# Turning more probability tiles by DVE and DRAM instead of TensorE, in a top-k attention and GELU kernel

## The chip, the cores and the metric

The kernel runs on 1 core of one Trainium2 chip. A core has five engines with a queue of instructions each, worked in order: TensorE (PE in the profile, its weight loads PEld), VectorE (DVE), ScalarE (ACT), GpSimd (POOL) and SyncE (SP, which here only issues DMAs). [...] The metric is device microseconds of one execution: the kernel before takes 1480.06 us (median of 3 runs, 1479.93 to 1480.07).

## The reference

Attention over 8 batches of 8 heads, 576 rows of 64 columns each, in which each row keeps its 32 largest scores; the heads of a batch are laid side by side and go through two products with an exact GELU between them. All is float32.

```python
scores = scale * np.matmul(q, k.transpose(0, 1, 3, 2))     # (8, 8, 576, 576)
kth = np.partition(scores, -32, axis=-1)[..., -32:-31]
scores = np.where(scores >= kth, scores, -1000000000.0)
scores = scores - np.max(scores, axis=-1, keepdims=True)
attn = np.exp(scores)
attn = attn / (np.sum(attn, axis=-1, keepdims=True) + 1e-09)
out = np.matmul(attn, v)
x = out.transpose(0, 2, 1, 3).reshape(4608, 512)
h = x @ w_in                                                # 512 x 2048
g = 0.5 * h * (1.0 + erf(h * inv_sqrt2))
return g @ w_out                                            # 2048 x 512
```

## The kernel before, in words

**Items.** The work of attention is cut into 144 items, 18 for each batch. An item is a tile `s` of 128 rows by 2 x 576 scores. 16 items of a batch are main items: 128 query rows of a pair of heads (a pair has 4 such blocks of rows, 512 in all; two neighbouring items, an even and an odd one, share a pair). The last 64 rows of the heads are left over, and two items of last rows hold them, each for two pairs (four heads). In even batches the items of last rows stand at the end, in odd batches at the start, so they come in groups of four.

**One step.** The order of instructions is written out by hand in one loop over n, and each engine takes its share in that order. In step n the loop makes the scores of item n + 2 (in even steps of n + 2 and n + 3, lines 386 and 394), the top-k of item n, the softmax of item n - 1, the transposes of item n - 2 and the product with v (`attend`) of item n - 3. Between them stand pieces of the two big products (`mlp`), lines 773 and 929 above all; `room_in` says how many pieces a step gets. Pieces are taken in a fixed order, and only when the rows of x that they need are there.

**Top-k.** DVE finds the 32 largest of a row in four rounds of 8 (line 483), and between rounds replaces those found by a very low number (line 486). For most items the first two rounds run over 288 larger halves (line 422), the last two over 576 numbers. In step n the last thing of the top-k is `last()`, the reciprocal of the sum of the exponentials of item n - 1 (line 504); DVE waits there for ACT's exponentials (line 529) by way of a small addition on POOL (line 510). After it POOL makes the threshold of item n (lines 497 and 498), which ACT needs for its selection (line 517), and multiplies item n - 1 by the reciprocal (line 552).

**Turning P.** The product with v needs the probabilities with the keys on the partitions, so each item is turned over. An ordinary item is turned by PE: one transpose for the 2 x 64 last keys (line 619) and eight for the rest (line 649), which ACT copies from PSUM to the tile `pt` (lines 629 and 664). An item of last rows needs two end transposes (line 622) and has a small tile `pt_end` of its own. Of the even main items 48 go another way (`squared`): DVE transposes all 32 x 32 squares of the tile in place (`square_p`, line 569, in the middle of the top-k two steps later), SP writes the tile to DRAM by four DMAs (`write_p`, line 579) and reads it back by four others in the order in which whole blocks are turned (`read_p`, line 586, at the head of the next step). The reads wait until the writes have landed. There is one tile `pt` (bufs=1); the even item fills its left half, the odd one its right half, and one product (line 715) takes both, in the step after the odd item's transposes.

**Loads.** From the fifth pair of heads on q and k are loaded in squares too, by eight DMAs for each of q and k of a pair (line 124), and DVE turns them (lines 284 to 288). All DMAs of the steady part are issued by SP, in program order; `issue` holds some back behind the write of a turned tile.

**Tiles.** Six tiles of scores `s` go round, so the scores of item n + 2 need the tile of item n - 4, in even steps those of n + 3 that of n - 3.

## Time and profile before

| what | value |
|---|---|
| median of 3 runs | 1480.06 us |
| profiled execution | 1479.73 us, span 1478.0 us |
| PE busy | 1461.6 us (99%) |
| DVE busy | 1294.3 us (88%) |
| POOL busy | 1140.1 us (77%) |
| ACT busy | 1099.9 us (74%) |
| DMA packets | 477645, 112.94 MB |
| DMA, queue of SP | 35.3% of 16 engines' span |
| granted PE clock | 1.00 |

Busy time of an engine is the time in which at least one of its instructions ran; a busy PE is not PE at its peak, since the ends of matmuls are modelled and overlap the next. A matmul of the program stands as two instructions in the trace, a transpose by PE as one. A row of a group gives the line, the engine, the operation, the tile written and those read, the shape and the count, then busy time in us and the mean length of one in ns, then the time for which the engine idled before it and what ended that. A row in order of time gives start and length in us. Rows of waits say who waited for whom, how long in total, how often, and the longest.

### The profile page before, as it was taken

Reading aid. Unit: us, or ns where it says so; the run is one execution under the profiler, and the core shown is the slowest. Engines: PE = TensorE matmul, PEld = TensorE weight load, DVE = VectorE, ACT = ScalarE, POOL = GpSimd, SP = SyncE. Lnnn points to the kernel's source line nnn. Section 1 sums busy time; section 2 is a strip of 40 time slices with the busy share of each in tenths; the row PEclk is TensorE's granted clock in tenths of the full one; section 3 lists DMA queues with packets and bytes.
Section 4 is the critical chain, followed back from the end, with each engine's and each line's share of the span. In section 5 each row is a group of like instructions: output and inputs, shape, how many; then the busy total and the mean of one; then the engine's idle time right before and its main releaser. Section 6 shows DMA issues by size and latency. Waiting matters only on the chain. (4 is left out here: it accounts for less than half of the span.)

```text
span 1478.0 us, 27006 instructions
## 1 busy us (share of the span) xinstructions
PE 1461.6 (99%) x8817; PEld 1147.9 (78%) x8817; DVE 1294.3 (88%) x3318; ACT 1099.9 (74%) x1942; POOL 1140.1 (77%) x1291
## 2 busy tenths in 40 slices
PE   8999999999999999999999999999999999999999
PEld 6876677877777777887777778787777777787787
DVE  8999899999999988999999987999999997998701
ACT  7999977877777687777777778777777777776620
POOL 6877567877898879877898978886788887987732
PEclk9999999999999999999999999999999999999999
DMA  7424310045435322345534331345453421233300
GB/s 198 143 86 124 84 48 1 24 88 101 95 73 93 66 58 52 65 95 108 105 83 81 69 61 47 66 93 99 97 103 73 89 55 41 61 61 72 70 15 15
DMA packets 477645, 112.94 MB, mean 76 GB/s; under 512 B 413216, under 2 KB 469056, under 8 KB 477504
## 3 DMA queue, kind: packets, MB, share of 16 engines
q1 hardware_dynamic: 476240, 110.78, 35.3%
q8 instruction: 70, 1.15, 0.3%
q14 instruction: 71, 0.58, 0.1%
q10 hardware_dynamic: 1200, 0.39, 0.1%
q0 software_dynamic: 64, 0.03, 0.0%
HBM read 73.39 MB, written 37.75 MB: 75 GB/s over the span
## 5 line engine op out<-in xcount | busy, mean ns | idle before, releaser
L773 PE MATMUL h_ps<-xT,w_in_sb 128*128 128x256 f32 (+1 forms) x2560 | 536.2, 361 | 0.1
L773 PEld LDWEIGHTS h_ps<-xT,w_in_sb 128*128 128x128 f32 x2560 | 436.5, 190 | 73.4 <-issue 25.2
L483 DVE MAX8 top<-lists 128x8 f32<-128x576 f32 (+1 forms) x792 | 476.4, 641 | 0.0
L486 DVE MATCH_REPLACE8 lists<-top,lists 128x288 f32<-128x288 f32 (+1 forms) x528 | 307.9, 589 | 0.0
L552 POOL TENSOR_TENSOR s<-s,rden 128x1152 f32<-128x1152 f32 x135 | 285.8, 2117 | 0.3 <-DVE rden L504 0.3
L529 ACT ACTIVATE s<-s,bias 128x576 f32<-128x576 f32 x288 | 225.4, 787 | 11.0 <-issue 0.4
L517 ACT ACTIVATE s<-s,neg 128x576 f32<-128x576 f32 x288 | 225.5, 793 | 1.7 <-POOL neg L497 1.6
L510 POOL TENSOR_SCALAR den<-den 128x2 f32<-128x2 f32 x144 | 31.4, 218 | 215.9 <-ACT s L529 210.2
L455 POOL TENSOR_TENSOR lists<-lists 128x576 int32<-128x576 int32 x132 | 186.2, 1410 | 4.0
L447 POOL TENSOR_TENSOR lists<-s 128x576 int32<-128x576 int32 x133 | 187.2, 1407 | 0.0
L715 PE MATMUL o<-pt,raw_v 128*64 128x256 f32 x1280 | 153.0, 384 | 1.8 <-ACT s L529 1.1
L715 PEld LDWEIGHTS o<-pt,raw_v 128*64 128x64 f32 x1280 | 87.8, 136 | 85.8 <-issue 37.2
L789 ACT ACTIVATE g<-h_ps 128x512 f32<-128x512 f32 x144 | 78.2, 594 | 100.6 <-PE h_ps L773 100.4
L929 PE MATMUL y_ps<-w_out_sb,sum 128*128 128x256 f32 x472 | 140.4, 379 | 0.0
L394 ACT ACTIVATE s<-s_ps 128x1024 f32<-128x1024 f32 x127 | 125.5, 1035 | 10.5 <-PE s_ps L386 10.3
L664 ACT COPY pt<-tp 128x1024 f32<-128x1024 f32 x85 | 86.6, 1019 | 62.2 <-PE tp L649 62.1
L386 PE MATMUL s_ps<-kt,qm 64*128 64x512 f32 x512 | 129.4, 618 | 0.8 <-ACT s L392 0.8
L504 DVE RECIPROCAL rden<-den 128x2 f32<-128x2 f32 x144 | 23.2, 161 | 108.6 <-POOL den L510 107.4
L486 DVE MATCH_REPLACE8 lists<-first,lists 128x288 f32<-128x288 f32 x264 | 114.3, 439 | 0.0
L929 PE MATMUL y_ps<-w_out_sb,g 128*128 128x256 f32 x480 | 113.4, 379 | 0.0
L483 DVE MAX8 first<-lists 128x8 f32<-128x288 f32 x268 | 106.6, 436 | 0.0
L929 PEld LDWEIGHTS y_ps<-w_out_sb,g 128*128 128x128 f32 x480 | 91.2, 190 | 12.4
(167 smaller groups left out, 2533.1 us busy)
## 6 DMA issues: line engine op xcount, KB each, us to landing
turned<-s SPq DMA_DIRECT2D x192, 144.0 KB, 3.5
pt<-turned SPq DMA_DIRECT2D x192, 144.0 KB, 3.2
raw_v<-in_v_dram SPq DMA_DIRECT2D x64, 128.0 KB, 2.4
out_dram<-y SPq DMA_DIRECT2D x30, 256.0 KB, 2.1
raw_q<-in_q_dram SPq DMA_DIRECT2D x112, 64.0 KB, 2.0
raw_k<-in_k_dram SPq DMA_DIRECT2D x112, 64.0 KB, 2.0
w_out_sb<-in_moe_w_in_dram SPq DMA_DIRECT2D x14, 511.8 KB, 4.8
w_out_sb<-in_moe_w_out_dram SPq DMA_DIRECT2D x10, 511.8 KB, 4.1
```

Source lines behind the costliest of these rows:

```text
L386: nc.tensor.matmul(s_ps[:, e], lhsT=q_t[rows, :], rhs=kt[rows, 0:SM], start=True, stop=True)
L394: nc.scalar.activation(spread(s, S + TL, SM), s_ps, func=AF.Copy, scale=scale)
L447: nc.gpsimd.tensor_tensor(t[:, :, 1].bitcast(i32), a.bitcast(i32), b.bitcast(i32), op=ALU.add)
L455: nc.gpsimd.tensor_tensor(into_of(i)[:, :, 1].bitcast(i32), both, top, op=ALU.subtract)
L483: nc.vector.max(x[:, e], src[:, e])
L486: nc.vector.match_replace(dst[:, e], x[:, e], src[:, e], LOWEST)
L517: nc.scalar.activation(s, s, func=AF.Prelu, bias=st["neg"][:, e : e + 1], scale=1.0, alpha=STEEP)
L529: nc.scalar.activation(s, s, func=AF.Exp, bias=st["bias"][:, e : e + 1], scale=1.0, accum_out=st["den"][:, e : e + 1],)
L552: nc.gpsimd.tensor_tensor(s, s, wide, op=ALU.mult)
L715: nc.tensor.matmul(o[e * D : (e + 1) * D, 0:n], lhsT=vt[:, j, e, :], rhs=pt[:, e * NJ + j if j < NM else NM, :], start=(j == 0), stop=(j = ...
L773: nc.tensor.matmul(h_tile(u)[:, i, :], lhsT=w_in_sb[:, ko, f * P : (f + 1) * P], rhs=xT[:, ko, c0 : c0 + n], start=(ko == 0), stop=(ko == ...
L929: nc.tensor.matmul(acc[names][:, k], lhsT=lhsT, rhs=rhs, start=(j == 0 and k == 0), stop=(j == FT // 2 - 1 and k == 1),)
```

## The change

- **More items turned by DVE and DRAM.** Beside the even main items from the 27th item on, `squared` now takes all 12 later items of last rows (`delayed`) and 16 odd main items (`later`: those whose place in a period of 36 items is 3, 13, 21, 25 or 29). PE's transposes and ACT's copies of these go; DVE gets a transpose of squares, SP four writes and four reads for each.
- **A layout for that.** For pairs loaded in squares the first head's left-over keys are its first 64 and not its last 64, so that an item of last rows has the same column layout as a main item, with the left-over keys of both heads side by side; `pt_end` goes. q and k take four DMAs each, not eight.
- **The later items' chain.** In the step after a later item the reciprocal is taken before the last maximum and not after it, and POOL multiplies before it makes the threshold. The square transpose stands after the first round of the top-k and not before the third. The product with v of a later item stands at the end of its step and not at the start, and two pieces of the big products are moved from the step before into that step (`bare`).
- **The delayed items.** Their products come one or two steps later, the two groups of an odd batch share a PSUM tile and one copy, and the small loads of v behind them are issued by ACT.
- **Room.** Seven tiles `s` in place of six; small tiles are put together, `part` has two buffers, `top` 16 columns.

```diff
--- before.py
+++ after.py
@@ -118,20 +118,24 @@
             for e in range(2):
+                at = e * TL if n == "k" else 0
                 for d in range(2):
                     rows, cols = slice((2 * e + d) * SQ, (2 * e + d + 1) * SQ), slice(d * SQ, (d + 1) * SQ)
-                    for at, lo, hi, by in ((0, 0, SM, queue), (SM + e * TL, SM, S, queue2)):
-                        by.dma_start(
-                            out=t[rows, at : at + hi - lo].rearrange("i (c j) -> i c j", j=SQ),
-                            in_=src[b, h0 + e, lo:hi, cols].rearrange("(c i) j -> i c j", i=SQ),
-                        )
+                    queue.dma_start(
+                        out=t[rows, at : at + S].rearrange("i (c j) -> i c j", j=SQ),
+                        in_=src[b, h0 + e, :, cols].rearrange("(c i) j -> i c j", i=SQ),
+                    )
             return
...
         for e in range(2):
+            end = TL if pair >= SQUARES and e == 0 else S
+            main = end % S
             queue.dma_start(
-                out=t[:, 0:NM, e, :], in_=src[b, h0 + e, 0:SM].rearrange("(t p) d -> p t d", p=P)
+                out=t[:, 0:NM, e, :], in_=src[b, h0 + e, main : main + SM].rearrange("(t p) d -> p t d", p=P)
             )
-            queue2.dma_start(out=t[e * TL : (e + 1) * TL, NM, e, :], in_=src[b, h0 + e, SM:S])
+            rows = slice(0, TL) if n == "q" else slice(e * TL, (e + 1) * TL)
+            queue2.dma_start(out=t[rows, NM, e, :], in_=src[b, h0 + e, end - TL : end])
...
@@ -283,7 +287,7 @@
             elif c == 1:
-                nc.vector.transpose(kt[:, q_tail:], rq[:, SM:])
+                nc.vector.transpose(kt[:, q_tail : q_tail + TL], rq[:, SM:S])
             else:
...
@@ -312,15 +316,33 @@
             if c != 0 and done >= {1, 2}:
-                load("q", pair + ahead)
+                issue(lambda: load("q", pair + ahead))
             if (c == 0 if pair >= SQUARES else c != 0 and done >= {0, 1, 2}):
-                load("k", pair + ahead)
+                issue(lambda: load("k", pair + ahead))
...
     S_of, stat_of = {}, {}
+    def main_keys(pair):
+        return slice(TL, TL + SM) if pair >= SQUARES else slice(0, SM)
+    def end_keys(pair, e):
+        at = e * (SM + TL) if pair >= SQUARES else SM + e * TL
+        return slice(at, at + TL)
+    def both_ends(pair):
+        kt = kt_of[pair]
+        return spread(kt, SM + TL, TL) if pair >= SQUARES else kt[:, SM : SM + P]
+    def end_rows(pair, e):
+        return slice(SM + P, SM + P + TL)
...
@@ -361,21 +379,19 @@
                 nc.tensor.matmul(
-                    t_ps[half(r, e), r * TL : (r + 1) * TL],
-                    lhsT=kt[:, SM + P + e * TL : SM + P + (e + 1) * TL],
-                    rhs=kt[:, SM + e * TL : SM + (e + 1) * TL],
+                    t_ps[half(r, e), e * TL : (e + 1) * TL],
+                    lhsT=kt[:, end_rows(pair + r, e)], rhs=kt[:, end_keys(pair + r, e)],
                     start=True, stop=True,
...
         return lambda: nc.scalar.activation(
-            s.rearrange("p (r n) -> p r n", r=2)[:, :, SM:S],
-            t_ps[:, 0:P].rearrange("p (r n) -> p r n", r=2), func=AF.Copy, scale=scale,
+            s[:, SM : S + TL], t_ps[:, 0:P], func=AF.Copy, scale=scale
         )
...
         pair, t = items[i]
-        S_of[i] = s = work.tile([P, 2 * S], f32, tag="s", bufs=6, name="s")
+        S_of[i] = s = work.tile([P, 2 * S], f32, tag="s", bufs=7, name="s")
         s_ps = pair_tile("s_ps", "l1" if second else "pr")
@@ -384,7 +400,7 @@
                 nc.tensor.matmul(
-                    s_ps[:, e], lhsT=q_t[rows, :], rhs=kt[rows, 0:SM], start=True, stop=True
+                    s_ps[:, e], lhsT=q_t[rows, :], rhs=kt[rows, main_keys(pair)], start=True, stop=True
                 )
...
@@ -454,18 +469,18 @@
-    def top_k(i, last, middle):
+    def top_k(i, last, middle, early, late):
...
             "first": work.tile([P, 2, 8], f32, tag="first", name="first"),
-            "neg": work.tile([P, 2], f32, tag="neg", name="neg"),
-            "bias": work.tile([P, 2], f32, tag="bias", name="bias"),
-            "den": work.tile([P, 2], f32, tag="den", name="den"),
-            "rden": work.tile([P, 2], f32, tag="rden", name="rden"),
         }
-        top = work.tile([P, 2, TOPK - 8], f32, tag="top", bufs=1, name="top")
-        into = [st["first"]] + [top[:, :, 8 * r : 8 * r + 8] for r in range(TOPK // 8 - 1)]
+        stat = work.tile([P, 4, 2], f32, tag="stat", name="stat")
+        st.update((n, stat[:, x]) for x, n in enumerate(("neg", "bias", "den", "rden")))
+        top = work.tile([P, 2, 16], f32, tag="top", bufs=1, name="top")
+        into = [st["first"]] + [
+            top[:, :, 8:16] if r == TOPK // 8 - 1 else top[:, :, 0:8] for r in range(1, TOPK // 8)
+        ]
         if paired(i):
@@ -477,17 +492,21 @@
         for r, (src, dst, x) in enumerate(rounds):
-            if 16 * r == TOPK:
+            if 16 * r == TOPK and not late:
                 middle()
...
                 nc.vector.max(x[:, e], src[:, e])
+                if early and e == 0 and r == len(rounds) - 1:
+                    last()
+            if r == 0 and late:
+                middle()
             if r < len(rounds) - 1:
...
                     nc.vector.match_replace(dst[:, e], x[:, e], src[:, e], LOWEST)
-            if r == len(rounds) - 1:
+            if r == len(rounds) - 1 and not early:
                 last()
-        st["kth"] = top[:, :, TOPK - 9]
+        st["kth"] = top[:, :, 15]
...
@@ -552,14 +571,26 @@
     pt_now = [None]
-    pt_end = const.tile([P, 2, P], f32, name="pt_end")
-    nc.gpsimd.memset(pt_end, 0.0)
...
-        return SINGLE.stop - 2 < i < N - 2 and i % 2 == 0 and items[i][1] < NM and i % RINGS != 12
+        if not SINGLE.stop - 2 < i < N - 2:
+            return False
+        return items[i][1] == NM or (i % RINGS in LATER if i % 2 else i % RINGS != 12)
+    def later(i):
+        return i % 2 == 1 and squared(i) and items[i][1] < NM
+    def delayed(i):
+        return squared(i) and items[i][1] == NM
+    def pt_tile():
+        return work.tile([P, 2 * NM + 1, 2 * P], f32, tag="pt", bufs=1, name="pt")
     RINGS = 2 * len(items) // B
+    LATER = (3, 13, 21, 25, 29)
     turned = {}
@@ -582,9 +613,12 @@
             d = turned.pop(i)
+            if i % 2 == 0:
+                pt_now[0] = pt_tile()
+            cols = slice(i % 2 * P, (i % 2 + 1) * P)
             for k in range(P // SQ):
                 nc.sync.dma_start(
-                    out=pt_now[0][k * SQ : (k + 1) * SQ, :, 0:P], in_=d[:, :, k, :]
+                    out=pt_now[0][k * SQ : (k + 1) * SQ, :, cols], in_=d[:, :, k, :]
                 )
...
@@ -615,32 +648,16 @@
                     )
-            elif t < NM:
+            else:
                 nc.tensor.transpose(tp[:, at : at + P], s[:, SM : S + TL], ident)
-            else:
-                for r in range(2):
-                    nc.tensor.transpose(
-                        tp[0:TL, at + r * P : at + (r + 1) * P],
-                        s[:, r * S + SM : (r + 1) * S], ident,
-                    )
             if keys:
                 keys()
-            if t < NM:
-                nc.scalar.copy(
-                    out=pt_now[0][:, NM, t % 2 * P : (t % 2 + 1) * P], in_=tp[:, at : at + P]
-                )
-                return
-            for e in range(2):
-                c = slice(e * TL, (e + 1) * TL)
-                nc.scalar.copy(
-                    out=halves(pt_end[c, 0, :], e, P),
-                    in_=halves(tp[0:TL, at : at + 2 * P], e, P),
-                )
-        x = t % 2 * P if t < NM else 0
+            nc.scalar.copy(out=pt_now[0][:, NM, x : x + P], in_=tp[:, at : at + P])
+        x = i % 2 * P
         def turn_over(tp, e):
-            first = e * (S + TL if t < NM else S)
+            first = e * (S + TL)
             for j in range(NM):
...
@@ -702,7 +721,9 @@
         pt = pt_now[0]
-        o = bank("o")
+        both = delayed(i) and i - 1 in starts
+        o = shared.pop() if both else bank("o")
+        off = 2 * TL if both else 0
         n, row = (2 * P, (t - 1) * P) if t < NM else (TL, SM)
@@ -724,18 +745,23 @@
                         nc.tensor.matmul(
-                            o[e * D : (e + 1) * D, r * TL : (r + 1) * TL], lhsT=vt[:, j, e, :],
-                            rhs=pt[:, r * NJ + j, half(r, e)] if j < NM else pt_end[:, r, half(r, e)],
+                            o[e * D : (e + 1) * D, off + r * TL : off + (r + 1) * TL],
+                            lhsT=vt[:, j, e, :],
+                            rhs=pt[:, e * NJ + j if j < NM else NM, i % 2 * P :][:, half(r, e)],
                             start=(j == 0), stop=(j == NJ - 1),
                         )
-            copies.append(lambda: nc.scalar.copy(
-                out=xT[:, at : at + 2, c],
-                in_=o[:, 0 : 2 * TL].rearrange("p (r n) -> p r n", r=2),
-            ))
+            if delayed(i) and i in starts:
+                shared.append(o)
+            else:
+                first = 0 if both else at
+                copies.append(lambda: nc.scalar.copy(
+                    out=xT[:, first : at + 2, c],
+                    in_=o[:, 0 : off + 2 * TL].rearrange("p (r n) -> p r n", n=TL),
+                ))
...
             for r in range(2 if t == NM else 1):
-                issue(lambda r=r: load("v", pair + r + NP))
+                issue(lambda r=r: load("v", pair + r + NP, None, nc.scalar if delayed(i) else None))
         if at == (NP - 1 if t < NM else NP - 2):
...
@@ -1088,6 +1113,10 @@
+    def bare(n):
+        return (n - 4 in starts and delayed(n - 4)) or later(n - 3)
     def room_in(n):
@@ -1095,7 +1124,7 @@
             return 0
-        return sizes[x] + (1 if x % 2 == 0 else -1)
+        return sizes[x] + (1 if x % 2 == 0 else -1) + 2 * (bare(n) - bare(n + 1))
@@ -1154,7 +1183,9 @@
         held[0] = n < N and squared(n - 2)
-        read_p(n - 3)
+        mid = [i for i in (n - 5, n - 4) if delayed(i) and n % 2 and (i % 2 or i in starts)]
+        if not mid:
+            read_p(n - 3)
         left[0] = room_in(n)
@@ -1175,7 +1206,10 @@
             scores(n + 3)
-        product = attend(n - 3)
+        if delayed(n - 4) and n % 2 == 0 and n - 4 not in starts:
+            product = attend(n - 4)
+        else:
+            product = not delayed(n - 3) and not later(n - 3) and attend(n - 3)
         late = n > START
@@ -1209,6 +1243,11 @@
             softmax(n - 1, 0)
+            if mid:
+                for i in mid:
+                    attend(i)
+                copy_x()
+                read_p(n - 3)
             if n % 2:
@@ -1248,18 +1287,26 @@
         run_gelus()
+        if later(n - 3):
+            attend(n - 3)
+            copy_x()
         if n < N:
-            top_k(n, lambda: inverse(n - 1), lambda: square_p(n - 2))
+            top_k(
+                n, lambda: inverse(n - 1), lambda: square_p(n - 2), later(n - 1), later(n - 2)
+            )
             write_p(n - 2)
...
             inverse(n - 1)
+        if later(n - 1):
+            normalise(n - 1)
         threshold(n)
...
             smaller(1)
-        normalise(n - 1)
+        if not later(n - 1):
+            normalise(n - 1)
         sum_up(n + 2)
@@ -1277,6 +1324,7 @@
         if n == 5:
+            nc.vector.memset(flat["k"][0][TL:, 0:TL], 0.0)
             load("q", SQUARES)
...
```

36 lines of the change are left out of this document (16 added, 20 removed).

## The prediction

> **What bounds the kernel now.** I read the busy shares first, then windows, then the waits, then the order of time around one item. The busy shares, then three stretches (columns of these: length, busy time of PE, its weight loads, DVE, ACT, POOL, clock, DMA share, GB/s):
>
> ```profile
> PE 1461.6 (99%) x8817; PEld 1147.9 (78%) x8817; DVE 1294.3 (88%) x3318; ACT 1099.9 (74%) x1942; POOL 1140.1 (77%) x1291
> ```
>
> ```profile
> 549.07:897.15 348.08, 347.57 (x2089) 273.51 (x2087) 321.91 (x832) 262.84 (x470) 286.56 (x322) 1.00 0.40 79
> 277.13:1406.19 1129.06, 1126.26 (x6732) 889.41 (x6729) 1033.55 (x2674) 847.60 (x1512) 921.95 (x1039) 1.00 0.39 77
> 1406.19:1478.00 71.81, 67.95 (x328) 58.49 (x326) 4.90 (x12) 12.05 (x27) 21.69 (x29) 0.99 0.04 15
> ```
>
> The first stretch is one period of 36 items (two batches). In it PE idles half a microsecond and DVE 348.08 - 321.91 = 26.2. The second holds every item that the change touches; the last is product work after the last item and is untouched. So PE sets the time, and DVE is close behind. Where DVE waits (total, times, longest), and one wait of the DMA queue:
>
> ```profile
> DVE rden L504 <- POOL den L510: 107.4, 92, 9.7
> ```
>
> ```profile
> SPq L586 <- DMA turned<-s: 95.2, 64, 4.0
> ```
>
> DVE's slack is spent at one place, the reciprocal that ends each item's top-k; I count a step of DVE from one reciprocal to the next. The second row is the read-back of a turned tile, which waits until the write of the same tile has landed.
>
> **What goes from PE.** The transposes of an ordinary item, and the end transposes of an item of last rows, in order of time (start, length, engine, line; the last number counts instructions):
>
> ```profile
> 715.87 0.27 PE L619 MATMUL tp_t<-ident,s 128*128 128x128 f32 x1
> 715.98 0.60 PE L929 MATMUL y_ps<-w_sum,sum 128*128 128x256 f32 x2
> 716.42 0.59 PE L929 MATMUL y_ps<-w_out_sb,sum 128*128 128x256 f32 x2
> 716.85 1.04 PE L649 MATMUL tp<-ident,s 128*128 128x128 f32 x8
> 717.72 0.60 PE L929 MATMUL y_ps<-w_sum,g 128*128 128x256 f32 x2
> ```
>
> ```profile
> 1259.92 0.38 PE L622 MATMUL tp_t<-ident,s 128*64 128x128 f32 x2
> 1260.13 0.60 PE L929 MATMUL y_ps<-w_sum,sum 128*128 128x256 f32 x2
> ```
>
> The lengths overlap, so I take start to next start: 715.98 - 715.87 = 0.11 for the end transpose and 717.72 - 716.85 = 0.87 for the eight main ones, 0.98 for a main item; 0.21 + 0.87 = 1.08 for one of last rows. The two programs' lists of instructions show 16 main items and 12 of last rows leaving PE (696 main transposes become 472); 4 earlier items of last rows stay and need one end transpose instead of two. Sum: 16 x 0.98 + 12 x 1.08 + 4 x 0.10 = 15.7 + 13.0 + 0.4 = 29.1 us. Busy time of the group gives another bound:
>
> ```profile
> L649 PE MATMUL tp<-ident,s 128*128 128x128 f32 x696 | 90.4, 273 | 0.0
> ```
>
> That is 0.130 a transpose, 224 x 0.130 = 29.1 for the main ones alone in place of 28 x 0.87 = 24.4, hence about 34 in all. It counts pipeline ends under which the next product already runs, so I take 29.1. The products behind the last item are equally many in both programs, so the final 71.8 us stays.
>
> [...]
>
> **What is added to DVE, and moved off ACT.**
>
> ```profile
> L664 ACT COPY pt<-tp 128x1024 f32<-128x1024 f32 x85 | 86.6, 1019 | 62.2 <-PE tp L649 62.1
> ...
> L569 DVE STREAM_TRANSPOSE s<-s 128x1152 f32<-128x1152 f32 x48 | 65.5, 1364 | 0.0
> ...
> L286 DVE STREAM_TRANSPOSE kt<-raw_q 128x128 f32<-128x128 f32 x28 | 8.2, 292 | 0.8 <-DMA raw_q<-in_q_dram 0.8
> ```
>
> 28 more squares cost DVE 28 x 1.364 = 38.2. The q piece shrinks from 128 to 64 columns; between none and half of its 0.292 comes back, I take 0.1, 28 x 0.1 = about 3. In a period that is 9 x 1.364 - 0.8 = 11.5 more for DVE while PE loses 5 x 0.98 + 4 x 1.08 = 9.2, so DVE's 26.2 of slack falls to 26.2 - 11.5 - 9.2 = 5.5. The inverse moved ahead of the last maximum asks for the sum 0.7 earlier (half of the last row of the next DVE fence), 5 x 0.7 = 3.5 a period, still inside. I cost DVE at nothing, but only 2 us a period of cover is left; beyond it each microsecond counts 1129/348 = 3.2 times. ACT loses 28 copies of 1.019 and was not the bound: nothing. The normalisation put ahead of the threshold delays ACT's selection by one multiplication on POOL, at most the 2.1 that the end of the square's input needs anyway; ACT is 74% busy and does that work a step ahead, so nothing, else 16 x 2.1 = 34 on DVE's chain.
>
> **What is added to the way through DRAM.** One even item before, from its step's start to its product: DVE, SP and PE in turn, and the time from a read's issue to its landing (the last number).
>
> ```profile
> 702.04 0.17 DVE L504 RECIPROCAL rden<-den 128x2 f32<-128x2 f32 x1 [0.68 <-POOL den L510]
> 702.12 0.76 DVE L422 TENSOR_TENSOR lists<-s 128x576 f32<-128x576 f32 x1
> 702.81 0.30 DVE L286 STREAM_TRANSPOSE kt<-raw_q 128x128 f32<-128x128 f32 x1
> 703.03 0.67 DVE L288 STREAM_TRANSPOSE qm<-raw_q 128x512 f32<-128x512 f32 x1
> 703.63 0.77 DVE L483 MAX8 first<-lists 128x8 f32<-128x288 f32 x2
> ...
> 706.74 1.36 DVE L569 STREAM_TRANSPOSE s<-s 128x1152 f32<-128x1152 f32 x1
> 708.03 1.37 DVE L483 MAX8 top<-lists 128x8 f32<-128x576 f32 x2
> ```
>
> ```profile
> 708.17 3.35 SPq L579 DMA_DIRECT2D turned<-s  x4
> ...
> 714.76 2.58 SPq L586 DMA_DIRECT2D pt<-turned  x4
> ```
>
> ```profile
> 700.74 1.99 PE L386 MATMUL s_ps<-kt,qm 64*128 64x512 f32 x8
> ...
> 718.68 1.99 PE L386 MATMUL s_ps<-kt,qm 64*128 64x512 f32 x8
> 720.60 2.38 PE L715 MATMUL o<-pt,raw_v 128*64 128x256 f32 x20
> ```
>
> ```profile
> 702.90 2.10 POOL L552 TENSOR_TENSOR s<-s,rden 128x1152 f32<-128x1152 f32 x1
> ```
>
> ```profile
> pt<-turned SPq DMA_DIRECT2D x192, 144.0 KB, 3.2
> ```
>
> The square ends at 708.10, the reads are issued by 717.34, and the last, issued at about 716.7, lands 3.2 later at 719.9: a trip of 11.8, and the product at 720.60 comes only 0.7 behind it. This trip has little slack already.
>
> For a moved odd main item the product stands at the end of PE's next step, behind the scores (720.60 - 718.68 = 1.92) and, by the list, 18 products at 0.44 (716.42 - 715.98) and one keys product of about 0.2: 10.0 into that step. Count from the reciprocal that opens the item's own step: PE is 1.3 ahead (702.04 - 700.74), a step is (348.08 - 9.2)/36 = 9.4, and two pieces of product work, 4 x 0.44 = 1.7, have left this step for the next. The product is due at -1.3 + 9.4 - 1.7 + 10.0 = 16.4. The square now stands behind the last maximum of the item before, the larger halves and the first maxima: 0.7 + 0.8 + 0.8 + 1.36, and as the reciprocal itself moved 0.7 ahead it ends about 3.0 after the old mark. POOL's 2.10, begun at the early reciprocal, is over just in time. But SP still holds the reads of the even partner: that square ended 6.06 - 0.8 = 5.3 into its own step (without q transposes), its reads are issued 9.2 later, so SP is free at 5.3 + 9.2 - 9.4 = 5.1 and the write starts 2.1 late. Data are there at 3.0 + 2.1 + 11.8 = 16.9. PE would wait 0.5; with ends of that kind uncertain by 0.2 I take 0.65 at each of the 16: 10.4 us. The bounds are 0 (PE later against DVE than in this one step) and 2 (DVE another 1.3 behind after heavy steps): 0 to 32. The value is nearest to the low end because the nearest row, the even item's product, came after its data.
>
> The 12 items of last rows have their products moved one or two steps later, so that a trip of 11.8 lies under about 18 us: nothing, at most 12 x 0.65 = 8. The queue's own account, by issue times (shortest/median/longest, ns):
>
> ```profile
> L579 SPq DMA_DIRECT2D turned<-s x192: 564/746/1987, 302.5 to 1387.1; - x192
> ```
>
> ```profile
> L586 SPq DMA_DIRECT2D pt<-turned x192: 567/604/1378, 308.6 to 1392.8; - x192
> ```
>
> ```profile
> L124 SPq DMA_DIRECT2D raw_q<-in_q_dram x224: 311/480/1992, 58.1 to 1202.2; - x112
> ```
>
> 112 more writes and 112 more reads cost SP 112 x (0.746 + 0.604) = 151; 224 fewer loads of q and k give 224 x 0.48 = 108 back. Behind a waiting read on SP stand the next loads of q, k and v and the stores, whose users come steps later: nothing. 24 value loads go to ACT's queue, 24 x 0.5 = 12 of ACT's idle time, and ACT waits there for a product that its next copy waits for too. The seventh tile of scores keeps score copies from waiting for a tile that now leaves by DMA; shared small tiles save space and no time.
>
> **Sum.** -29.1 + 10.4 = -18.7. The profiled execution took 1479.73 against a median of 1480.06, a difference too small to matter: 1480 - 19 = 1461.
>
> **Rivals.** (1) The whole gain: the trip stays hidden, 1480 - 29 = 1451; for it, the even items' data came in time; against it, a margin of 0.7. With the larger bound, 34, it would be 1446. (2) DVE becomes the bound: if half of its 26.2 of waiting stays where it is, a period is 321.9 + 11.5 + 13 = 346.4, the gain 1.7 x 3.2 = 5, the time 1475. For it, the wait hangs on ACT's exponentials, which keep PE's pace; against it, the wait should go as DVE falls behind. (3) The other side: three turned tiles in a row on one queue lengthen the trip by 2 us. Then PE waits 2.65 at 16 products, 42 us, and the time is 1480 - 29 + 42 = 1493. It decides from 29.1/16 = 1.8 a product. For it, the write queued behind its partner's reads; against it, fewer loads in the queue, and DMA engines 40% busy on average. [...]
>
> **Chances.** A difference under 0.2% (3 us) can't be told from none. My forecast, 1454 to 1469: 0.50. Rival 1, 1445 to 1454: 0.17. Rival 2 and mixtures, 1469 to 1477: 0.14. Rival 4 or an exact balance: 0.05. Rival 3: 0.14. Faster is then 0.81, the same 0.05, slower 0.14. The range of 1447 to 1477 leaves out rival 3, rival 4 and the very best, about 2 in 10.
>
> **What would show it.** After the change: 472 main transposes on PE and about 29 us less of its busy time; 76 squares on DVE near 1.36; DVE near 91% busy, (1294.3 + 38.2 - 3)/1461, and its wait at the reciprocal well under 107; PE idle of about 10 us in front of the odd items' products, ended by the DMA of the read. The prediction is wrong if PE waits over 1.8 at each of those products, or if it waits for ACT's copies held up by late thresholds.

## The result, and the profile after

The kernel after takes 1538.88 us (median of 4, 1537.16 to 1539.78) beside 1480.07 us for the kernel before on the same chip: a ratio of 1.0396 with a 95% interval of 1.0378 to 1.0414. It is 59 us slower, where 19 us less had been forecast. The profiled execution took 1539.1 us, with a span of 1537.3.

The busy shares of the kernel after, first; then windows of it (length, busy time of PE, its weight loads, DVE, ACT, POOL, clock, DMA share, GB/s), three short ones behind waits of PE and one period of 36 items:

```profile
PE 1455.7 (95%) x8549; PEld 1131.9 (74%) x8549; DVE 1350.8 (88%) x3347; ACT 1064.5 (69%) x1867; POOL 1141.9 (74%) x1290
```

```profile
425.10:428.50 3.40, 3.40 (x17) 2.31 (x19) 3.40 (x9) 0.00 (x0) 2.91 (x5) 0.50 0.88 138
524.10:530.90 6.80, 5.00 (x24) 2.75 (x28) 6.80 (x16) 0.37 (x1) 3.74 (x6) 0.50 0.41 70
592.40:599.20 6.80, 4.42 (x45) 3.98 (x46) 6.80 (x18) 3.30 (x5) 3.60 (x4) 0.50 0.75 125
657.50:1025.74 368.24, 346.13 (x2000) 269.21 (x1998) 339.80 (x841) 251.69 (x447) 286.90 (x322) 0.98 0.52 104
```

A period grew from 348.08 to 368.24 us. DVE's busy time in it grew by 339.80 - 321.91 = 17.9, and its idle time did not shrink: 26.2 before, 368.24 - 339.80 = 28.4 now. PE's idle time grew from 0.5 to 22.1, and in short stretches the clock was granted at half (0.50 in the three windows), which makes its busy time longer too: a product below took 4.06 us in place of 2.38.

The waits of PE and of DVE (total, times, longest), and four groups of instructions:

```profile
PE o L736 <- DMA pt<-turned: 40.3, 19, 4.7
PE o L747 <- DMA pt<-turned: 14.4, 4, 4.5
```

```profile
DVE stat L523 <- POOL stat L529: 103.4, 84, 10.0
```

```profile
L571 POOL TENSOR_TENSOR s<-s,stat 128x1152 f32<-128x1152 f32 x135 | 285.9, 2118 | 10.6 <-DVE stat L523 10.6
L437 DVE TENSOR_TENSOR lists<-s 128x576 f32<-128x576 f32 x133 | 122.8, 924 | 0.6
L600 DVE STREAM_TRANSPOSE s<-s 128x1152 f32<-128x1152 f32 x76 | 103.6, 1363 | 0.0
L666 PE MATMUL tp<-ident,s 128*128 128x128 f32 x472 | 61.3, 273 | 0.0
```

PE waits 54.7 us for tiles read back from DRAM, in the products of main items (line 736) and of last rows (747). The 224 transposes are gone and the 76 squares took 1.363 us each, as forecast. DVE still waits 103.4 us at the reciprocal. The mean of the larger halves (line 437) rose; the same group before:

```profile
L422 DVE TENSOR_TENSOR lists<-s 128x576 f32<-128x576 f32 x133 | 100.8, 758 | 0.0
```

That is 22.0 us more of DVE for the same 133 instructions. Where it comes from, and how the trip of an odd item runs, shows in order of time (start, length, engine, line; the wait before it in brackets):

```profile
407.42 2.11 POOL L571 TENSOR_TENSOR s<-s,stat 128x1152 f32<-128x1152 f32 x1 [0.28 <-DVE stat L523]
408.03 2.11 DVE L437 TENSOR_TENSOR lists<-s 128x576 f32<-128x576 f32 x1
408.22 2.54 SPq L620 DMA_DIRECT2D pt<-turned  x4
410.80 1.35 DVE L600 STREAM_TRANSPOSE s<-s 128x1152 f32<-128x1152 f32 x1
412.23 3.72 SPq L610 DMA_DIRECT2D turned<-s  x4
...
418.69 0.76 DVE L437 TENSOR_TENSOR lists<-s 128x576 f32<-128x576 f32 x1
419.64 2.10 POOL L571 TENSOR_TENSOR s<-s,stat 128x1152 f32<-128x1152 f32 x1
419.78 2.79 SPq L620 DMA_DIRECT2D pt<-turned  x4
...
425.07 4.06 PE L736 MATMUL o<-pt,raw_v 128*64 128x256 f32 x20 [2.59 <-DMA pt<-turned]
```

In the step of an odd item POOL multiplies while DVE makes the larger halves of the next list, and these take 2.11 instead of the 0.76 us of the step behind, where POOL multiplies after them. They end at 410.14, 0.61 after the multiplication, which itself takes its usual 2.11: only DVE pays. (2.11 - 0.76) x 16 = 21.6 explains the group's 22.0. The square ends at 412.15, the reads are issued from 419.78 and landed by 424.9: a trip of 12.8 us against the 11.8 forecast, and a wait of 2.59 against 0.65. The product behind it took 4.06 us, 3.4 of them at half clock, where one of the same shape took 2.38 before.

### The profile page after: what moved, and what is told of

Its sections match the earlier page's. It is cut to its first block, busy times and chain, and to the rows that moved or that the text cites. A ratio compares the mean times of both kernels' runs of the same rounds, so it can differ in the third digit from the quotient of the medians.

```text
span 1537.3 us, 26403 instructions
## 1 busy us (share of the span) xinstructions
PE 1455.7 (95%) x8549; PEld 1131.9 (74%) x8549; DVE 1350.8 (88%) x3347; ACT 1064.5 (69%) x1867; POOL 1141.9 (74%) x1290
## 5 line engine op out<-in xcount | busy, mean ns | idle before, releaser
L571 POOL TENSOR_TENSOR s<-s,stat 128x1152 f32<-128x1152 f32 x135 | 285.9, 2118 | 10.6 <-DVE stat L523 10.6
L536 ACT ACTIVATE s<-s,stat 128x576 f32<-128x576 f32 x288 | 224.2, 785 | 54.2 <-POOL stat L516 54.0
L548 ACT ACTIVATE s<-s,stat 128x576 f32<-128x576 f32 x288 | 224.4, 782 | 10.7
L736 PE MATMUL o<-pt,raw_v 128*64 128x256 f32 x1280 | 163.8, 404 | 42.6 <-DMA pt<-turned 40.3
L529 POOL TENSOR_SCALAR stat<-stat 128x2 f32<-128x2 f32 x144 | 31.4, 218 | 223.9 <-ACT s L548 208.1
L736 PEld LDWEIGHTS o<-pt,raw_v 128*64 128x64 f32 x1280 | 96.9, 144 | 120.5 <-issue 77.7
L410 ACT ACTIVATE s<-s_ps 128x1024 f32<-128x1024 f32 x127 | 124.6, 1027 | 12.6 <-PE s_ps L402 10.5
L741 ACT COPY xT<-o 128x256 f32<-128x256 f32 x64 | 24.4, 381 | 148.8 <-PE o L736 148.8
L516 POOL TENSOR_SCALAR stat<-top 128x2 f32<-128x2 f32 x144 | 68.5, 476 | 78.2 <-DVE stat L523 68.2
L437 DVE TENSOR_TENSOR lists<-s 128x576 f32<-128x576 f32 x133 | 122.8, 924 | 0.6
L523 DVE RECIPROCAL stat<-stat 128x2 f32<-128x2 f32 x144 | 22.8, 158 | 103.8 <-POOL stat L529 103.4
```

Of the source, the lines that this page charges most:

```text
L410: nc.scalar.activation(spread(s, S + TL, SM), s_ps, func=AF.Copy, scale=scale)
L536: nc.scalar.activation(s, s, func=AF.Prelu, bias=st["neg"][:, e : e + 1], scale=1.0, alpha=STEEP)
L548: nc.scalar.activation(s, s, func=AF.Exp, bias=st["bias"][:, e : e + 1], scale=1.0, accum_out=st["den"][:, e : e + 1],)
L571: nc.gpsimd.tensor_tensor(s, s, wide, op=ALU.mult)
L736: nc.tensor.matmul(o[e * D : (e + 1) * D, 0:n], lhsT=vt[:, j, e, :], rhs=pt[:, e * NJ + j if j < NM else NM, :], start=(j == 0), stop=(j = ...
```

## The experiments

Two theories stood against each other at first. Theory 1: PE's waits for the trip are the loss, and the half clock behind them makes it larger. Theory 2: DVE is the loss, by the larger halves held up and by squares that it has no room for. All times are medians beside runs of the kernel before (1480.07 to 1480.85 us), with the ratio's 95% interval.

**One part alone.** Last rows only, odd items only, and neither (the layout, four DMAs for q or k, seven tiles stay):

```diff
-    LATER = (3, 13, 21, 25, 29)
+    LATER = ()                                # rows only, and neither
...
-        return items[i][1] == NM or (i % RINGS in LATER if i % 2 else i % RINGS != 12)
+        if items[i][1] == NM:
+            return False                      # odd only, and neither
+        return i % RINGS in LATER if i % 2 else i % RINGS != 12
```

> Of the change only the 12 items of last rows are turned by DVE and DRAM; the 16 odd main items go back to PE. Theory 1 (PE waits for tiles that come back from DRAM, and its clock is halved behind the longer waits): PE loses 13 us of transposes, keeps the 16 us of waits at products of last rows and some 8 us of half clock, so about 1490. Theory 2 (DVE is held up, since the early multiplication on POOL collides with the larger halves, 16 times about 1.4 us): no early multiplication is left, so 1467 to 1470.

> Only the 16 odd main items are turned by DVE and DRAM; items of last rows go back to PE. Theory 1: 16 us of transposes go, waits of 33 us at odd products and up to 9 at even ones stay, with some 15 us of half clock, about 1515 to 1522. Theory 2: 16 us go and 22 us of DVE's hold-ups stay, about 1486.

> No further item is turned by DVE and DRAM; the new layout, four loads for q or k, held behind the writes, seven tiles of scores and shared small tiles stay. Both theories: within 3 us of the kernel before, 1477 to 1482, with no half clock. A time over 1485 would put part of the loss on the loads or the layout.

Measured: rows only 1509.27 (1.0174 to 1.0208), odd only 1526.62 (1.0300 to 1.0334), neither 1490.38 (1.0052 to 1.0082). All three lie above what either theory gave. Both parts lose, and 10 us are lost without either. For those 10 us one even item of the run with neither, in order of time:

```profile
670.59 1.36 DVE L602 STREAM_TRANSPOSE s<-s 128x1152 f32<-128x1152 f32 x1
672.01 4.75 SPq L612 DMA_DIRECT2D turned<-s  x4
676.81 2.77 SPq L124 DMA_DIRECT2D raw_k<-in_k_dram  x4
...
683.30 2.59 SPq L622 DMA_DIRECT2D pt<-turned  x4
...
688.78 1.52 PE L738 MATMUL o<-pt,raw_v 128*64 128x256 f32 x12 [2.48 <-DMA pt<-turned]
```

Four loads of k, which `issue` now holds back to the end of the step, stand on SP between the write and the read of an even item, in front of loads of v and two stores that stand there in the kernel before too. The write's issue ends at 676.76, and such writes land 3.5 us after their issue (median of the 192), but the read is issued at 683.30; from the square's end at 671.95 to the product are 16.8 us, and PE waits 2.48.

**Loads of q and k not held back.**

```diff
-                issue(lambda: load("q", pair + ahead))
+                load("q", pair + ahead)
...
-                issue(lambda: load("k", pair + ahead))
+                load("k", pair + ahead)
```

> No further item turned by DVE and DRAM (as in e3_neither), and the loads of q and k are issued at once again, not held behind the write of a turned tile. Theory 1 (SP's order: a held load stands between a tile's write and its read, the read is late, PE waits): the 13 us of waits at even products go, 1477 to 1481. Theory 2 (the layout, the seventh tile or the larger loads cost the 10 us): stays at 1488 to 1491.

> The whole change, but the loads of q and k are issued at once, not held. Theory 1: the 9 us of waits at even products go and a few at odd ones, with them some half clock, 1515 to 1530. Theory 2: no change, 1537 to 1540.

> Only items of last rows turned by DVE and DRAM, q and k loaded at once. Theory 1: as e1_rows_only less 12 us of waits at even products and the half clock behind them, 1490 to 1500; the waits at last rows of 16 to 20 us stay. If the held loads did not matter here: 1505 to 1510.

> Only the 16 odd main items turned by DVE, q and k loads at their place in the order (not held for the end of a step), last rows by PE. It is the base for the two runs beside it. With the held loads this part alone took 1526.6 us, and taking the hold away gave 6 to 16 us elsewhere: both theories say 1512 to 1522 us.

Measured: neither 1479.05 (0.9980 to 0.9999), the whole change 1532.54 (1.0313 to 1.0384), rows only 1492.98 (1.0069 to 1.0103), odd only 1516.67 (1.0225 to 1.0261). The first, third and fourth came as theory 1 or both theories had it; the whole change lies between the two. The hold is worth 11.3, 6.3, 16.3 and 10.0 us in the four; the 6.3 is hardly clear of noise, since the intervals with and without it overlap. Layout and seventh tile are free. On this base the last rows cost 13.9 and the odd items 37.6 us; both together with 1479.05 make 1530.6, so the parts add.

The trace of the last rows alone shows where their 13.9 us lie. Beside the run with neither, one step in each of three groups of last rows grows, from 8.25 us to 14.86, 16.67 and 15.77, and all other steps together gain 9.0 us (13.0 forecast). In the long steps PE waits for the fourth item of the group. The first of the three, in order of time:

```profile
556.58 6.55 SPq L134 DMA_DIRECT2D raw_v<-in_v_dram  x4
559.52 1.36 DVE L600 STREAM_TRANSPOSE s<-s 128x1152 f32<-128x1152 f32 x1
563.31 2.63 SPq L620 DMA_DIRECT2D pt<-turned  x4
566.36 3.66 SPq L610 DMA_DIRECT2D turned<-s  x4
573.81 2.62 SPq L620 DMA_DIRECT2D pt<-turned  x4
579.50 2.40 PE L747 MATMUL o<-pt,raw_v 128*64 128x64 f32 x40 [4.07 <-DMA pt<-turned]
590.02 0.17 DVE L523 RECIPROCAL stat<-stat 128x2 f32<-128x2 f32 x1 [6.74 <-POOL stat L529]
```

The square ends at 560.88, its write starts 5.5 us later, behind the read of the item before and loads of v, and the tile is back 18.5 us after the square. DVE idles 6.74 us in this step, so it is not the bound there. Behind the wait the clock was granted at 0.50 from 579.1 to 582.5, and for 6.8 us in the other two steps. The wait and half of such a stretch make 5.8 us where the step grew by 6.6, and 7.7 where the others grew by 8.4 and 7.5. That fits a half clock that costs time, but no run tried it apart.

**The chain not moved forward**, in the whole change: reciprocal behind the last maximum, square late, multiplication behind the threshold, for all items.

```diff
-                n, lambda: inverse(n - 1), lambda: square_p(n - 2), later(n - 1), later(n - 2)
+                n, lambda: inverse(n - 1), lambda: square_p(n - 2), False, False
...
-        if later(n - 1):
-            normalise(n - 1)
...
-        if not later(n - 1):
-            normalise(n - 1)
+        normalise(n - 1)
```

> The whole change, but the later items' chain is not moved forward: reciprocal, multiplication and square stand where they stand for other items. Theory 1: the squares end 2 to 3 us later, PE waits that much longer at 16 products, so 1565 to 1590. Theory 2: the collision of multiplication and larger halves is gone, 16 x 1.4 = 22 us less, about 1517.

Measured 1538.89 (1.0375 to 1.0406), the time of the change itself; both theories missed. Moving the chain forward gives nothing here. What it gains and what it loses is separated only by the old tile below.

**Filling PE's waits** with products that nobody reads (the only work added; it goes to an unused part of the tile `o`), to keep the clock up:

```diff
+        for _ in range(5 if later(i) else 10 if both else 0):
+            nc.tensor.matmul(o[:, 2 * P : 4 * P], lhsT=ident, rhs=w_out_sb[:, 0, 0 : 2 * P], start=True, stop=True)
```

> The whole change; in front of each product of a later item PE multiplies 5 times (2.2 us) and in front of the second product of an odd batch's last rows 10 times (4.3 us) into an unused part of the product's PSUM tile; the results are not used. Theory 1 with the clock as a cost of its own: the extra matmuls fill most of PE's waits, no half clock is granted there, so 24 us less half clock and little added, 1515 to 1528. If PE's clock is not on the path: 1537 to 1550, since the extra work costs up to 16 x 2.2 + 3 x 4.3 = 48 where there is no wait.

Measured 1534.73 (1.0347 to 1.0384). A window of the kernel after and the same of this run (the clock is the third number from the end):

```profile
560.00:600.00 40.00, 33.72 (x281) 27.62 (x280) 37.78 (x91) 23.82 (x41) 34.50 (x39) 0.91 0.68 140
```

```profile
560.00:600.00 40.00, 37.39 (x270) 29.27 (x270) 37.05 (x87) 24.84 (x42) 33.03 (x40) 1.00 0.72 152
```

Summed over the traces, the stretches of half clock shrank from 47.8 to 8.1 us, PE's idle time between 280 us and the last item from 67.7 to 31.3, and the time by 4 us, with intervals that touch. If half clock cost half its length, 20 us should have come back. The time lies between what the two readings gave. So the half clock is not shown to be a cost of its own of that size; as the filler takes PE's time too, the run can't say that it is none.

**Other places for loads and products**: loads of v on ACT's queue; four pieces of product work moved before each later product, in the whole change and with odd items alone; six, with odd items alone and the chain not moved forward. All with q and k not held.

```diff
-                issue(lambda r=r: load("v", pair + r + NP, None, nc.scalar if delayed(i) else None))
+                load("v", pair + r + NP, nc.scalar)
...
-        return sizes[x] + (1 if x % 2 == 0 else -1) + 2 * (bare(n) - bare(n + 1))
+        return sizes[x] + (1 if x % 2 == 0 else -1) + 2 * (bare(n) - bare(n + 1)) + 4 * (later(n - 3) - later(n - 4))
```

> The whole change with loads of q and k issued at once, and all loads of v of the steady part issued by ACT. Theory 1 (SP's queue holds up writes and reads around the items of last rows, where trips take 18 us): trips fall to 12 to 14 us, the waits of 16 us at last rows mostly go, 1490 to 1510. If the trip is long because the DMA engines are full, not SP: no better than with SP, 1515 to 1530.

> The whole change with q and k loaded at once, and four pieces of product work (3.5 us of PE) moved from behind each later item's product to in front of it, within the same two steps. Theory 1 (only the place of the product in PE's order makes PE wait): most of the 33 us of waits at odd products go, those at last rows (20) stay, 1495 to 1510. Theory 2 (DVE is the bound, it has 38 us more of squares and 22 us of collisions with POOL, and PE's waits only show that): no change, 1528 to 1540.

> Only odd main items turned by DVE and DRAM, q and k loaded at once, the four pieces moved as in e9. Theory 1: the waits at odd products nearly vanish, 1465 to 1480. Theory 2: stays near e2_odd_only less its even waits, 1510 to 1525.

> As e10, but the later items' chain is not moved forward (no early reciprocal, multiplication behind the threshold, square in the ordinary place), and six pieces are moved. If the collision of the early multiplication with the larger halves is a cost of its own (16 x 1.4 us on DVE), this is faster than e10 by up to 20 us, 1460 to 1470; if not, the later square makes PE wait again, 1480 to 1500.

Measured: 1555.40 (1.0459 to 1.0529), 1567.17 (1.0569 to 1.0601), 1557.85 (1.0509 to 1.0540), 1533.13 (1.0341 to 1.0371). Each missed, and why the first two are so slow was not traced. The last, with the chain not moved forward, lies 24.7 below the third, where up to 20 had been expected. The largest waits of PE in the third, odd items with four pieces moved:

```profile
PE tp_t L654 <- POOL s L571: 30.4, 10, 6.5
PE seven L955 <- POOL g L840: 24.2, 13, 2.8
...
PE o L738 <- DMA pt<-turned: 1.5, 4, 0.6
```

The wait for the read is nearly gone, and PE waits for POOL's multiplication and sums instead. A product that doesn't wait for the trip was no gain here; but the moved pieces made these other waits themselves, so the run does not decide against theory 1.

**An old tile.** To take the trip away, odd items read a tile written once, beside the first turned item, so that their output is that of an old tile; squares, writes and reads are all issued. In the first pair the read stays behind its own write on SP, in the second it is issued a step earlier, with the even item's. Each pair is run with the chain moved forward and not.

```diff
             d = turned.pop(i)
+            if later(i):
+                d = old[0]
...
             d = turned.pop(i)
+            if later(i):
+                return
             if i % 2 == 0:
                 pt_now[0] = pt_tile()
+                read_old(i + 1)
```

> As the run beside it, but the odd items' reads take an older tile in DRAM, written once long before, so the product of an odd item waits for no trip of its own; square, writes and reads are all issued as before (its output holds old weights for the odd items, so it is not the reference's). Theory 1: the trip through DRAM is what the odd items cost; without it the 16 us of transposes are gained and the time is 1460 to 1472 us. Theory 2: the squares and the early multiplication load DVE and POOL beyond their slack, whatever the trip does; the time stays at 1500 us or more, and PE waits for copies, sums and multiplications instead of the read.

> As the run before, with the odd items' chain not moved forward (square before the 25th to 32nd largest's first search is done for no item early, multiplication after the threshold for all); the odd items' output is again that of an old tile. Theory 1: as the run before, 1460 to 1472 us. Theory 2 in its narrow form, that the early multiplication's collision with the larger halves is the loss: 16 times 1.35 us less on DVE, so 15 to 25 us below the run before. Theory 2 in its wide form, that DVE has no room for 16 more squares of 2.3 us: 1495 us or more here too.

> The runs before, that read an old tile, still held the odd item's read on SP behind the write that waits for the odd item's own square, and PE still waited 13 to 15 us for it. Here the old tile is read a step earlier, with the even item of the pair, so that the odd product waits for no square and no DMA; squares, writes, reads and the early multiplication stay (the odd items' output is again that of an old tile). If the early multiplication is a loss of its own (by it the larger halves take 2.1 instead of 0.76 us, and thresholds come later): 1480 to 1492 us, that is 10 to 20 us below the run that waited, and 15 to 25 us above the run beside this one. If all of the loss was the wait of PE: 1460 to 1466 us in both.

> As the run beside it with the odd items' chain not moved forward (the odd items' output is that of an old tile). What is left is the load: 16 squares more on DVE, 16 turns fewer on PE, 64 writes and 64 reads more. If DVE has room for the squares: 1461 to 1468 us, that is 14 to 16 us of wait less than the run that waited 14.6 us. If it has none, the gain on PE is lost again: 1473 to 1482 us.

Measured: 1502.15 (1.0129 to 1.0163) and 1481.64 (0.9997 to 1.0015); read ahead, 1502.07 (1.0129 to 1.0159) and 1478.68 (0.9974 to 0.9993). The first and the last came as theory 2 had it, the second as its narrow form (a square takes 1.37 us, not the 2.3 named there); the third missed. The pair with the read ahead gives three prices. The trip: 1516.67 - 1502.07 = 14.6. The chain moved forward, which is three moves at once: 1502.07 - 1478.68 = 23.4. And with both gone the 16 odd items gain 0.4 us on 1479.05, where 15.7 had been taken from PE.

The 0.4 holds a loss that belongs to the experiment. The first odd item reads the old tile just after it was written, and holds up its neighbours on SP (run with the read ahead, nothing moved forward):

```profile
306.01 4.31 SPq L617 DMA_DIRECT2D old<-s  x4
313.82 2.80 SPq L625 DMA_DIRECT2D pt<-old  x4
316.68 2.55 SPq L640 DMA_DIRECT2D pt<-turned  x4
...
338.52 3.73 PE L757 MATMUL o<-pt,raw_v 128*64 128x256 f32 x20 [3.50 <-DMA pt<-turned]
```

By the reciprocals of the traces this run is 0.6 us behind the run without odd squares at item 31 and 4.7 behind at item 36, but 0.6 ahead at the last item: the other fifteen odd items gain 5.3 us of the 14.7 taken from PE. The run from which the trip's 14.6 is taken has the same loss, so that the trip itself is nearer 18 or 19.

In the first pair PE still waited 12 to 15 us for the old tile, since the read stands behind the write that waits for the item's square. From item 36 on these are 10.5 us of wait with the chain moved forward and 12.7 without, and they cost 2.2 and 5.8 us of time: a wait of PE is paid in part.

One step of DVE from reciprocal to reciprocal, the same item in three runs: with no odd squares; with squares, read ahead and nothing moved forward; and with the chain moved forward too.

```profile
653.22 0.15 DVE L523 RECIPROCAL stat<-stat 128x2 f32<-128x2 f32 x1
...
662.76 0.17 DVE L523 RECIPROCAL stat<-stat 128x2 f32<-128x2 f32 x1 [1.41 <-POOL stat L529]
```

```profile
657.78 0.15 DVE L523 RECIPROCAL stat<-stat 128x2 f32<-128x2 f32 x1
...
661.72 1.37 DVE L602 STREAM_TRANSPOSE s<-s 128x1152 f32<-128x1152 f32 x1
...
667.08 0.15 DVE L523 RECIPROCAL stat<-stat 128x2 f32<-128x2 f32 x1
```

```profile
663.61 0.15 DVE L523 RECIPROCAL stat<-stat 128x2 f32<-128x2 f32 x1
...
664.45 2.11 DVE L437 TENSOR_TENSOR lists<-s 128x576 f32<-128x576 f32 x1
...
675.00 0.14 DVE L523 RECIPROCAL stat<-stat 128x2 f32<-128x2 f32 x1
```

The step takes 9.54, 9.30 and 11.39 us. In the first it has 1.41 of wait. The square fills that wait to the last, no wait is left at the reciprocal, and PE's shorter work can't make the step shorter than DVE's own 9.30. This item still gains 1.4 in all, the rest of it in the four steps behind, where DVE has waits. Moved forward, the step has a maximum (0.74) more, which its neighbour has less, and 1.35 more for the larger halves.

Not every wait at the reciprocal can be used. In the same step of items 39, 75 and 111 it falls from 2.17 to 0.94 and the step gets no shorter (10.26 and 10.30 at item 75). There DVE waits for POOL's own queue; item 75, nothing moved forward:

```profile
761.05 1.42 POOL L470 TENSOR_TENSOR lists<-lists 128x576 int32<-128x576 int32 x1
762.55 0.22 POOL L529 TENSOR_SCALAR stat<-stat 128x2 f32<-128x2 f32 x1
762.81 0.17 DVE L523 RECIPROCAL stat<-stat 128x2 f32<-128x2 f32 x1 [0.94 <-POOL stat L529]
```

The exponentials ended at 758.4; POOL comes to its small addition from other work without a break. In the kernel before, 40 of the 92 waits at the reciprocal, 39 of 107 us, are of this kind, and not for ACT.

**Squares alone.** Neither part, q and k not held, six tiles; 16 squares on DVE at the places of the odd items, from the weights into a tile that nobody reads.

```diff
     def square_p(i):
+        if SINGLE.stop - 2 < i < N - 2 and i % RINGS in (3, 13, 21, 25, 29):
+            nc.vector.transpose(idle_square, w_in_sb[:, 0, 0 : 2 * S])
```

> The kernel with neither kind of added squares and q and k loads at their place (1479.05 us), plus 16 squares of the same size on DVE at the places of the odd items, from the first layer's weights into a tile that nobody reads; six score tiles, as before, to make room. PE, ACT, POOL and the DMAs do no work more or less. If DVE's waits at the reciprocal, some 110 us in all, can take the squares: 1479 to 1484 us. If DVE's time adds to the end whatever it waits elsewhere: 16 times 1.25 to 1.36 us more, 1498 to 1502 us. Between the two, 1485 to 1497, where some of the steps concerned have a wait and the others none.

Measured 1479.69 (0.9983 to 1.0002) against 1479.05 without them: DVE's waits take the squares up. The windows of one period, the same 36 items, for neither; squares alone; odd items read ahead, not forward; the same, forward; and odd items with the trip:

```profile
634.47:982.29 347.82, 347.08 (x2080) 273.08 (x2079) 321.34 (x832) 261.60 (x465) 286.65 (x322) 1.00 0.40 79
```

```profile
635.05:983.07 348.02, 347.18 (x2079) 273.12 (x2078) 327.39 (x837) 261.68 (x466) 287.46 (x322) 1.00 0.40 79
```

```profile
639.02:984.99 345.97, 343.28 (x2034) 268.54 (x2033) 327.32 (x836) 255.94 (x456) 287.63 (x322) 1.00 0.50 97
```

```profile
645.51:999.50 353.99, 344.29 (x2034) 268.09 (x2033) 334.42 (x836) 256.54 (x455) 287.47 (x322) 1.00 0.49 95
```

```profile
648.69:1010.30 361.61, 349.36 (x2038) 271.93 (x2037) 334.45 (x836) 256.13 (x457) 287.24 (x322) 0.99 0.46 93
```

DVE's idle time per period is 26.5, 20.6, 18.7, 19.6 and 27.2. Squares alone are taken from the idle time. With the transposes gone from PE as well it falls to 18.7 and not to the 16 that a full gain would leave, and PE idles 2.7. The period is 1.85 shorter, where 4.9 had gone from PE. What goes on DVE after that is paid in full: 334.42 - 327.32 = 7.1 more of busy time, 8.0 more of time. With the trip DVE idles 7.6 more again; by what way PE's waits reach it was not traced.

## Why the prediction was wrong

**The step that failed** first is the one that set DVE's slack of a period against DVE's added work of a period: "so DVE's 26.2 of slack falls to 26.2 - 11.5 - 9.2 = 5.5. [...] I cost DVE at nothing". Slack is not pooled. The step shown had 1.41 us, which a square of 1.37 used up; in three steps the wait was for POOL and no use; and the early multiplication came on top of full steps. In place of 15.7 for the transposes of the odd items and 0 for moving the chain, the runs showed some 5 gained and 23.4 lost. The second is the trip of the last rows, put at nothing: 13.9 lost in place of 13.0 gained.

**The terms**, on the base with loads not held back, in us against 1480.07:

| step of the prediction | forecast | measured |
|---|---|---|
| layout, four DMAs, seventh tile | 0 | -1.0 |
| 16 odd items: transposes gone, squares added | -15.7 | -0.4 (some -5 without the old tile's first read) |
| reciprocal, multiplication and square moved ahead | 0 | +23.4 |
| odd items' trip | +10.4 (0 to 32) | +14.6 (18 to 19 likewise) |
| last rows, transposes and trip | -13.0 (to -5) | +13.9 |
| q and k held back by `issue` | not costed | +6.3 |
| sum | -18.7 | +56.8 |

The sum, with 0.4 forecast for four earlier items, comes within 2 us of the measured 58.8; the differences of two runs carry some 2 to 3 us each, the 6.3 some 6.

**The early multiplication.** I named what it delays, ACT's selection, and costed that at nothing, "else 16 x 2.1 = 34 on DVE's chain". What I did not see is that POOL's multiplication now stands beside the larger halves, the row behind the reciprocal in my own fence of the even item. The measured 23.4 answers to 16 x 1.35 = 21.6 on a DVE without slack; the later thresholds, moved by the same edit, were not tried alone. The trace shows the larger halves at 2.11 us beside the multiplication and at 0.76 without it; by what way POOL holds DVE up is not shown. Why the whole change without the move forward took the same 1538.89 stays open: the earlier square should save in the trip what the collision costs, but PE's waits for read tiles are only 61.2 there against 54.7.

**The trip.** Its mechanism was right and its size near: the term of 10.4 was 14.6 to 19, with trips of 11.3 to 19.1 us, 14.0 in the mean, in place of 11.8. That it came so near is partly luck. "The write starts 2.1 late" did not hold: nine of the sixteen writes start within 0.1 us of the square's end, as the one shown does, and three wait 6.3 to 7.3 behind the last rows' reads. In the change PE's waits at the odd products came to 32.7 us, summed from the trace, 2.0 each and not 0.65, but a wait of PE is not all time, as the old tile shows.

**The last rows.** "A trip of 11.8 lies under about 18 us: nothing, at most 12 x 0.65 = 8". In the kernel after the trips there reached 18.9, because the writes stood on SP behind reads and loads of v, and the reads behind loads of v and stores; with rows alone and loads not held, PE still waited at three of these products:

```profile
PE o L747 <- DMA pt<-turned: 12.7, 3, 4.3
```

The three steps with these waits lose 22.5 us and the others gain 9.0, which leaves the 13.9 but for 0.4. The steps that hold the squares are at most 0.2 us longer than without them, so the loss is the trip with the half clock behind it; at most the 4.0 us between the 9.0 and the 13.0 forecast can be DVE's load.

**SP.** "Behind a waiting read on SP stand the next loads [...] nothing" looked at the wrong side: the loads came to no harm, but the reads stood behind them.

**The rivals.** Rival 3 had the side and the place: PE waited over 1.8 us at ten of the sixteen odd products. It gave 1493, but more than half of the loss lay elsewhere, and even without the trip there was only a third of the gain. Rival 2, DVE the bound, was the nearest in its reason: half of the wait stays where it is, and in the odd items without trip and early multiplication 18.7 of 26.5 stay. It was priced at 1475 because the collision was not in it; and the wait did not hang on ACT alone, as it had it, but in part on POOL. Rival 4, no gain from PE's transposes (1480), fits the 1478.68 of the same run, but PE has no gaps to speak of for it: it idles 0.7 us in the period of 347.82 without odd squares.

**The signs.** The counts, 472 transposes and 76 squares of 1.36, came as named. PE's busy time fell by 5.9 and not by 29, with 47.8 us at half clock in it, DVE stayed at 88% in place of 91, and its wait at the reciprocal at 103.4.

## What to carry to other kernels

When one engine is at 99% and another at 88%, look at the second one's slack in each step that gets work, not in the period: here a wait of 1.41 us took a square of 1.37, and the step gained next to nothing from the first engine (9.54 to 9.30 us). Ask also whom the wait is for: one that a third engine's queue set was of no use in three steps here (10.26 and 10.30 us at item 75). Before moving an instruction, list what runs on the neighbour engine at its new place: here VectorE's larger halves took 2.11 us beside GpSimd's multiplication and 0.76 without it. On a DMA queue, cost what is issued between a write and its read-back, not only the trip itself: the loads of q and k held there cost 11.3 us here in the run with neither part.

## What was not expected of the hardware

The clock fell to half in stretches of 3.4 or 6.8 us at waits of PE of a few microseconds: waits of 2.34 and 2.59 us came with 3.4 us (694.8 to 698.2, 425.1 to 428.5), waits of 4.41 and 4.11 us with 6.8 (524.1 to 530.9, 592.4 to 599.2), one of 4.54 us with 3.4 (964.4 to 967.8), and waits of 1.83 and 2.86 us elsewhere with none. What sets the length, and which waits bring a stretch, is not shown: waits of 2.34 and 2.59 us were enough, and one of 2.86 was not.
